# Memory-augmented recurrent transformer with an MLP on one core: TensorE's unit order and the planner's priorities are given per place in a block

## The chip, the cores and the metric

The kernel runs on one core of one Trainium2 chip. The metric is the device time of one launch in microseconds (us). All times below are us unless they are marked ns.

## What is computed

The sequence has 2048 tokens of width 512 in 64 segments of 32 tokens. Each segment is attended to together with 8 memory rows, and the attention's output in these rows is the memory of the next segment, so the segments run one after the other. Then comes an MLP with residuals.

```python
def _A_ref(x, mem0, Wq, Wk, Wv, Wo, seg_len):        # x 1x2048x512, 32 heads of 128, 8 memory rows
    mask = (idx[:, None] < M) | (idx[:, None] >= idx[None, :])
    mem = mem0
    for s in range(n_seg):                            # 64 segments of 32 tokens
        h = jnp.concatenate([mem, xs], axis=1)        # 40 rows
        q, k, v = (jnp.einsum('btd,dhe->bhte', h, W) for W in (Wq, Wk, Wv))
        scores = jnp.where(mask, jnp.einsum('bhqe,bhke->bhqk', q, k) * scale, -1e9)
        o = jnp.einsum('bhqk,bhke->bhqe', _softmax(scores), v)
        o = jnp.einsum('bhte,hed->btd', o, Wo)
        mem = o[:, :M, :].copy()                      # the next segment's memory
        outs.append(o[:, M:, :])

h = x + _A_ref(_layernorm(x), A_mem0, A_Wq, A_Wk, A_Wv, A_Wo, 32)
h2 = h + (gelu(_layernorm(_layernorm(h)) @ w1 + b1) @ w2 + b2)   # w1 512x1792, w2 1792x512
```

## The kernel before

All four attention weights stay in SBUF in bf16. A row tile of 32 rows holds a segment's first 24 tokens and the 8 memory rows (pack A, tile hT); the last 8 tokens of four segments make another tile of 32 rows (pack B, tile hB). A *block* is four segments. Pack B of a block does not depend on the memory and is projected during the block before.

TensorE (PE) works in *units*. A projection pass, for instance Q0 (the first 16 heads of Q), is four units, one for each 128 of the 512 input columns; each unit is four matmuls that run side by side in four column tiles. Where two units in a row use the same columns of the same pack, the second leaves its weight loads out (those matmuls have line 453, the others 703). The parts of a segment and their lines:

| part | what | line |
|---|---|---|
| Q0, Q1, K0, K1, V0, V1 | projections of pack A, four units each | 703 or 453 |
| SC0, SC1 | scores of the rows that need memory or last tokens (the recurrent path) | 870 |
| PV0, PV1 | their probabilities times V | 901, 905 |
| SA, PVA | scores of the first 24 tokens, and their probabilities times V one segment later | 932, 962 |
| WO | output projection, eight units; units 0 to 3 read heads of PV0, 4 to 7 of PV1 | 990 |
| F0, F1 | filler that the recurrence does not wait for: pack B of the next block (K, Q, V at block positions 0, 1, 2), at position 3 the output projection of pack B (line 1019), in the last block the first products of the MLP (line 1140) | 703, 1019, 1140 |

Around them, ScalarE (ACT) and VectorE (DVE) copy results out of PSUM (kq, VS, OT, lines 721 and 722), DVE transposes (KALL and QT, line 746), and the softmax of SC runs as reduction (nmc, L879, DVE), Exp (EC, L883, ACT), reciprocal (rsc, L886), product (PC, L889) and transpose (PTC, L890, all DVE). After WO, DVE transposes the result (TT, L1002) and adds its halves into the next segment's hT (L996). The softmax of SA has lines 942 to 951.

A planner in the kernel sets the order. Every instruction is recorded with its reads and writes and an estimated duration. PE's order is written by hand: `ORDER` is a list of (part, first unit, end unit), the same for every segment from 1 on; segment 0 has its own list `START`. For the other engines, `Sched.schedule` goes through all instructions by rank (the longest estimated path to the end) plus a number from the table `BONUS` for the kind of tile written, and gives each the earliest gap on its engine. A copy that DVE or ACT can do goes to the one that would be done first. Waits come from the dependences; each engine then runs its list in order.

```python
ORDER = (("Q0", 0, 4), ("K0", 0, 4), ("Q1", 0, 4), ("K1", 0, 2), ("SC0", 0, 99), ("K1", 2, 4), ("V0", 0, 4), ("V1", 0, 2), ("SC1", 0, 99),
         ("V1", 2, 4), ("PVA", 0, 99), ("PV0", 0, 99), ("F0", 0, 2), ("WO", 0, 4), ("PV1", 0, 99), ("F0", 2, 4), ("WO", 4, 8), ("F1", 0, 4),
         ("SA", 0, 99))
```

`START` has two fillers ("W", 7, 8) of eight 512 column matmuls each (line 672) between the WO units of segment 0. The WO weights come in eight pieces, the last of the weight loads on SP's queue (line 630).

The MLP (phase 2) goes through four blocks of 512 tokens. Its first layer starts during the last block of segments: `w1_first` computes rows of it, some of them copied raw to SBUF and put through Gelu later (`gelu_late`, line 1154). `p2_norm` (L1091, DVE) normalizes a block of h, `p2_T` transposes it by DMA, `p2_res` (L1097, POOL) adds b2 to h. The blocks' inputs are loaded back from h_mid. Nothing but the reuse of the attention's weight buffers holds the norms and b2 sums of the first two MLP blocks back.

Of the kernel before, what the change touches and what calls it, by code (L numbers as in the profile page):

```python
# [32 lines left out]
HALVES = ("kq", "KA", "QT", "ZCm", "VS", "nmc", "EC", "rsc", "PC", "PTC", "OTm", "KB", "QTB", "VSB")  # L33
BONUS = {"": 40, "EC0": -0.86, "EC1": 0.35, "KA0": -40, "KA1": 2.87, "KB0": -40, "OTB": -0.07, "OTm0": 0.99, "OTm1": -3.04, "OTx": -40, "PA": -19.24,
# [18 lines left out]
START = (("B", "V", 0, (0, 6), (1, 7)), "V", "Y", "X", ("B", "V", 1, (0, 6), (1, 7)), ("B", "K", 0, (0, 4), (1, 6)), "K0", "K1", ("B", "K", 1, (0, 4), (1, 6)),
         ("B", "Q", 0, (0, 5)), "Q0", ("B", "Q", 0, (1, 4)), "Q1", "Z", "SC0", "SC1", ("B", "Q", 1, (0, 5)), "PV0", "PV1", "SA", "WO", ("T", "WO", 0, 2),
         ("B", "Q", 1, (1, 6)), ("T", "WO", 2, 4), ("W", 7, 8), ("T", "WO", 4, 6), ("W", 7, 8), ("T", "WO", 6, 8))


class Op:
    __slots__ = ("eng", "fn", "reads", "writes", "idx", "gidx", "deps", "sig", "sigcount", "waits",
                 "tag", "pad", "held", "name", "is_dma", "dma_sem", "dur", "mode", "alone", "rank", "start", "succ", "prev", "ni", "dma_count", "alts", "kind", "occ", "kb")  # L60

    def __init__(self, eng, fn, reads, writes, name, dur, mode):
        self.eng, self.fn, self.reads, self.writes = eng, fn, reads, writes
        self.name, self.dur, self.mode = name, dur, mode
# [12 lines left out]


class Sched:
# [391 lines left out]
def build_kernel(nc, A_x, A_mem0, A_Wq, A_Wk, A_Wv, A_Wo, B_w1, B_b1, B_w2, B_b2, out):  # L471
# [3 lines left out]
    with st:  # L475
# [446 lines left out]
        def sa_mm(s, bank):  # L922
# [165 lines left out]
        def p2_norm(k):  # L1088
            for t in range(TBS):
                tb = k * TBS + t  # L1090
                S.op("dve", lambda e, tb=tb, t=t: e.tensor_scalar(xn2[:, k % 2, t, :], hx_of(k)[:, t, :], agg2[:, tb, 0:1], rst2[:, tb:tb + 1], ALU.subtract, ALU.mult),  # L1091
                     reads=[("hx", k % 2), ("ag2", tb), ("rs2", tb)], writes=[("xn4", bf_of(k), t)], after=used["WV"], dur=0.4)

        def p2_res(k):

            for t in range(TBS):
                S.op("pool", lambda e, t=t: e.tensor_tensor(hb[:, k % 2, t, :], hx_of(k)[:, t, :], b2bc[:], ALU.add), reads=[("hx", k % 2), "b2bc"],  # L1097
                     writes=[("hb", k % 2, t)], after=used["WV"] + (S.users([("rs2", NTB - 1)]) if k else []), dur=1.1)

# [35 lines left out]
        def w1_first(fc, bank, raw=False):  # L1135
# [14 lines left out]

        def gelu_late(fc):
            g, gkeys = gT0_home[fc // 2]
            g = g[:, fc % 2, :]
            S.op("act", lambda e: e.activation(g, g, ACTF.Gelu_apprx_tanh, bias=b1t[:, fc:fc + 1], scale=1.0),
                 reads=["b1t"], writes=[("gT0", fc)] + gkeys, after=exps, dur=0.66)

# [322 lines left out]
```

## Time and profile before

| | us |
|---|---|
| median of 3 runs | 842.88 |
| lowest, highest | 841.43, 843.8 |
| the profiled execution | 842.46 |
| its span, first to last instruction | 840.7 |
| PE busy, DVE busy, ACT busy, POOL busy | 800.1, 577.3, 554.3, 91.6 |

The profile is of one execution. An instruction's row gives its start (from the span's start), its duration, engine, line, operation and the tiles (written <- read), then in brackets idle time of the engine just before it and what ended it. Rows with x16 merge 16 instructions. PEld are weight loads. Ends of matmuls are modelled and overlap the next start, so the start-to-start distances tell what a unit takes. A row of a stretch (A:B) gives its length and the busy time of PE, PEld, DVE, ACT and POOL with instruction counts, then the TensorE clock granted, the busy share of the DMA engines and GB/s.

### The profile page before, as it was taken

To read this page: it belongs to the slowest core of one execution; us is meant where nothing else is said; L and a number is where in the kernel's file an instruction comes from. 1 tells how busy PE (TensorE), PEld (TensorE's weight loads), DVE (VectorE), ACT (ScalarE), POOL (GpSimd) and SP (SyncE) were. 2 spreads that over 40 slices of the span, in tenths; PEclk is the share of its full clock that TensorE was granted. 3 is DMA by queue.
4 is the path that set the end of the run, shared out by engine and by line. 5 is a ranking of instruction groups with operands and counts; after the bars stand their busy time and mean duration, and the time that the engine had idled before them with its cause. 6 is when DMAs were issued, how large, how long until landed. Compare 5 with 4: busy or idle time off the path is not lost.

```text
span 840.7 us, 46469 instructions
## 1 busy us (share of the span) xinstructions
PE 800.1 (95%) x21625; PEld 396.3 (47%) x20613; DVE 577.3 (69%) x1920; ACT 554.3 (66%) x1504; POOL 91.6 (11%) x211
## 2 busy tenths in 40 slices
PE   3788999999999999999999999999999999999998
PEld 1344544445545445445444444444545454444443
DVE  3267778878787878787878787878787877742111
ACT  2546676777677777777767777777777776672332
POOL 5012000101010101010100101000000000102500
PEclk9999999999999999999999999999999999999999
DMA  9952010101010110101010101010121130274200
GB/s 345 388 158 23 4 35 5 44 15 35 24 36 24 28 32 26 33 23 36 23 36 25 35 25 35 18 29 25 41 44 35 37 98 11 69 196 94 76 26 25
DMA packets 66946, 48.75 MB, mean 58 GB/s; under 512 B 28980, under 2 KB 63164, under 8 KB 66748
## 3 DMA queue, kind: packets, MB, share of 16 engines
q1 hardware_dynamic: 66416, 45.50, 19.0%
q8 instruction: 165, 2.70, 1.4%
q14 instruction: 33, 0.27, 0.1%
q10 hardware_dynamic: 332, 0.27, 0.1%
HBM read 31.08 MB, written 8.13 MB: 47 GB/s over the span
## 4 chain that ended last, share of the span: by engine, by line
PE 79%; DVE 11%; ACT 4%; DMA 3%; SPq 2%; issue 1%; DVEq 0%
PE ps L703 35%; PE ps L990 11%; PE ps L453 7%; PE quad L1357 6%; PE ps L1350 4%; PE quad L901 3%; PE ps L1019 3%; DMA WQ<-in_A_Wq_dram 2%; SPq L615 2%; PE quad L962 2%; PE quad L870 2%; PE ps L932 2%; DVE opT L996 2%; DVE PC L889 1%; PE ps L870 1%
## 5 line engine op out<-in xcount | busy, mean ns | idle before, releaser
L990 PE MATMUL ps<-WO,OT 128*32 128x256 bf16 x4224 | 140.3, 274 | 3.2 <-ACT OT L721 1.5
L990 PEld LDWEIGHTS ps<-WO,OT 128*32 128x32 bf16 x4224 | 103.8, 96 | 52.3 <-ACT VS L721 26.6
L721 ACT CAST OT<-quad 128x128 bf16<-128x128 f32 (+1 forms) x130 | 68.3, 526 | 87.5 <-PE quad L905 86.9
L703 PE MATMUL ps<-WQ,hT 128*32 128x512 bf16 x1796 | 121.3, 383 | 3.4 <-DVE hT L996 3.2
L721 ACT CAST kq<-ps 128x512 bf16<-128x512 f32 x162 | 94.7, 585 | 42.1 <-PE ps L703 41.4
L703 PE MATMUL ps<-WK,hT 128*32 128x512 bf16 x1544 | 117.0, 379 | 0.0
L703 PE MATMUL ps<-WV,hT 128*32 128x512 bf16 x1528 | 116.8, 380 | 0.0
L722 ACT ACTIVATE kq<-ps 128x512 bf16<-128x512 f32 x160 | 94.5, 591 | 17.7 <-PE ps L703 17.1
L721 ACT CAST VS<-ps 128x512 bf16<-128x512 f32 x127 | 74.8, 589 | 12.9 <-PE ps L703 11.0
L768 POOL COPY ZC<-QTB 128x256 bf16<-128x256 bf16 x64 | 28.3, 442 | 498.3 <-PE ps L870 360.1
L746 DVE STREAM_TRANSPOSE KALL<-kq 128x256 f32<-128x256 f32 x160 | 69.0, 438 | 14.6 <-ACT kq L721 8.2
L1002 DVE STREAM_TRANSPOSE TT<-ps 128x256 f32<-128x256 f32 x66 | 29.7, 450 | 67.8 <-PE ps L990 66.4
L703 PEld LDWEIGHTS ps<-WQ,hT 128*32 128x32 bf16 x1796 | 44.7, 97 | 50.4 <-issue 20.9
L703 PEld LDWEIGHTS ps<-WV,hT 128*32 128x32 bf16 x1528 | 36.8, 97 | 56.1 <-issue 42.7
L703 PEld LDWEIGHTS ps<-WK,hT 128*32 128x32 bf16 x1544 | 38.0, 97 | 53.2 <-issue 39.5
L1353 ACT ACTIVATE WQ<-ps,b1t 128x512 bf16<-128x512 f32 x42 | 28.9, 687 | 49.9 <-PE ps L1350 49.9
L746 DVE STREAM_TRANSPOSE QT<-kq 128x256 f32<-128x256 f32 x128 | 56.4, 440 | 4.4 <-ACT kq L722 4.3
L453 PE MATMUL ps<-WV,hT 128*32 128x512 bf16 x520 | 51.3, 382 | 0.0
L944 ACT ACTIVATE SA<-SA 128x256 f32<-128x256 f32 x64 | 26.7, 417 | 35.9 <-DVE SA L943 35.9
L453 PE MATMUL ps<-WK,hT 128*32 128x512 bf16 x504 | 49.8, 379 | 0.0
L1420 DVE TENSOR_TENSOR WV<-quad,WV 128x512 bf16<-128x512 f32 x16 | 11.1, 691 | 54.4 <-PE quad L1357 54.4
L889 DVE TENSOR_TENSOR PC<-EC,rsc 128x128 bf16<-128x128 f32 x128 | 40.1, 313 | 4.3
(156 smaller groups left out, 1377.9 us busy)
## 6 DMA issues: line engine op xcount, KB each, us to landing
WV<-in_A_Wv_dram SPq DMA_DIRECT2D x4, 1024.0 KB, 10.4
WK<-in_A_Wk_dram SPq DMA_DIRECT2D x4, 1024.0 KB, 15.8
WQ<-in_A_Wq_dram SPq DMA_DIRECT2D x4, 1024.0 KB, 22.1
WO<-in_A_Wo_dram SPq DMA_DIRECT2D x8, 512.0 KB, 9.4
v_last<-VSB SPq DMA_DIRECT2D x60, 64.0 KB, 2.5
VBD<-v_last SPq DMA_DIRECT2D x60, 64.0 KB, 3.1
h_mid<-xr SPq DMA_DIRECT2D x16, 128.0 KB, 1.7
WQ<-h_mid SPq DMA_DIRECT2D x4, 512.0 KB, 4.3
```

What stands on the lines that cost most here:

```text
L453: return e.add_instruction(mybir.InstMatmult(name="I-%d" % (4000000 + _kept[0]), engine=mybir.EngineType.PE, start_tensor_calc=start, stop ...
L703: ins = e.matmul(o, l, m, start=(k == 0), stop=(k == DC - 1), tile_position=(0, 32 * j), skip_group_check=True)
L721: return {"act": (lambda e: e.copy(out, src), t_act(n, ps_)), "dve": (lambda e: e.tensor_copy(out, src), 0.16 + 1.042e-3 * n * fast)}
L722: return {"act": (lambda e: e.mul(out, src, scale_), t_act(n, ps_)), "dve": (lambda e: e.tensor_scalar(out, src, scale_, None, ALU.mult), ...
L746: S.op("dve", lambda e: e.transpose(out, src), reads=[("kq", i)], writes=[key], dur=t_dve(256) + 0.02, after=after)
L768: S.op("pool", lambda e: e.tensor_copy(dst, src), reads=[("QTB", bk % 2, q) for q in range(2)], writes=[("ZCb", par)], dur=0.45)
L889: S.op("dve", lambda e: e.tensor_tensor(PC[:, r].rearrange("p t a -> p a t"), EC[:, r], bc, ALU.mult), reads=[("EC", r), ("rsc", r)], writ ...
L990: ins = e.matmul(ps[bank][32 * j:32 * j + 32, 0:256], lhs(slot(h)), wo_cols(h, b), start=(k == 0), stop=(k == 15), tile_position=(0, 32 * ...
L1002: S.op("dve", lambda e: e.transpose(tt.rearrange("p c q t -> p (c q t)"), ps[bank][:, 0:256]), reads=[("ps", bank)], writes=[("TT", par)], ...
L1350: ins = e.matmul(ps[bank][:, 0:SBT], W1[:, cc, fc * P:(fc + 1) * P], hnT_of(k)[:, cc, :], start=(cc == 0), stop=(cc == DC - 1))
L1353: S.op("act", lambda e: e.activation(gT[:, fc, :], ps[bank][:, 0:SBT], ACTF.Gelu_apprx_tanh, bias=b1t[:, fc:fc + 1], scale=1.0), reads=[(" ...
L1357: S.op("pe", lambda e: e.matmul(quad[:, t, :], gT_of(k, fc)[:, t * P:(t + 1) * P], W2[:, fc, :], start=(fc == 0), stop=(fc == FC - 1)), re ...
```

## The change

- `ORDERS` gives PE's unit order for each place: segments 1 to 3 (a1 to a3), the four positions in a block for all later ones (m0 to m3), and the last four segments (z60 to z63). `ORDER` remains for the order of recording and for the direction in which a pass goes through the columns. A word such as K1.0.1 is units 0 to 1 of K1.
- `BONUS` may have a key with the position in the block ("EC0@2"), which goes before the plain one.
- `START` loses its two fillers.
- `p2_norm` now waits for the last segment's second PTC, `p2_res(0)` for the last PTA.
- The first late Gelu is planned with `TABLE` = 1.28 for the load of its table, and every other Gelu of the first MLP block comes after it. The planned duration of the product into PA becomes 0.418.
- `solo` is added and used by no instruction.

```diff
+TABLE = 1.28
...
-BONUS = {"": 40, "EC0": -0.86, "EC1": 0.35, "KA0": -40, "KA1": 2.87, "KB0": -40, "OTB": -0.07, "OTm0": 0.99, "OTm1": -3.04, "OTx": -40, "PA": -19.24,
...
+BONUS = {"": 1.48, "EC0": -6.96, "EC0@0": 40, "EC0@1": -40, "EC0@2": -4.22, "EC0@3": -16.94, "EC1": -5.94, "EC1@0": 1.8, "EC1@1": 8.6,
...
+ORDERS = {"a1": "Q0.0.2 K1.0.1 Q1.0.1 K0.0.1 Q0.2.4 K0.1.4 Q1.1.4 K1.1.3 SC0.0.1 K1.3.4 V1.0.1 SC0.1.2 V0.0.1 V1.1.2 V0.1.3 SC1.0.1 V1.2.4 V0.3.4 PVA.0.2 PV0.0.1 SA.0.1 WO.0.2 PV1.0.1 WO.2.8",
...
+          "m0": "Q0.0.3 K0.0.2 Q0.3.4 K0.2.4 Q1.0.4 K1.0.1 V1.0.1 K1.1.4 V0.0.1 SC0.0.1 V0.1.2 V1.1.2 V0.2.3 F0.0.1 V0.3.4 F0.1.2 SC1.0.1 V1.2.4 PVA.0.2 PV0.0.1 F0.2.4 WO.0.2 PV1.0.1 WO.2.8 SA.0.1 F1.0.4",
+          "m1": "K0.0.1 Q0.0.2 K0.1.2 Q0.2.4 Q1.0.1 K0.2.4 Q1.1.4 K1.0.1 V1.0.1 K1.1.3 SC0.0.1 K1.3.4 V0.0.3 V1.1.2 V0.3.4 V1.2.4 SC1.0.1 PVA.0.2 F0.0.1 PV0.0.1 F0.1.4 WO.0.2 PV1.0.1 WO.2.8 F1.0.3 SA.0.1 F1.3.4",
+          "m2": "Q0.0.2 K0.0.2 Q0.2.4 Q1.0.1 K0.2.4 Q1.1.3 K1.0.1 Q1.3.4 V1.0.1 K1.1.4 SC0.0.1 V0.0.3 V1.1.4 V0.3.4 SC1.0.1 F0.0.3 PVA.0.2 PV0.0.1 F0.3.4 F1.0.1 WO.0.2 PV1.0.1 WO.2.8 F1.1.3 SA.0.1 F1.3.4",
+          "m3": "Q0.0.4 K0.0.3 Q1.0.1 K0.3.4 Q1.1.3 K1.0.1 Q1.3.4 K1.1.4 SC0.0.1 V1.0.1 V0.0.3 V1.1.2 V0.3.4 SC1.0.1 V1.2.3 PVA.0.2 V1.3.4 F1.0.1 PV0.0.1 F1.1.4 WO.0.1 PV1.0.1 WO.1.8 F1.4.5 SA.0.1 F1.5.8",
...
-         ("B", "Q", 1, (1, 6)), ("T", "WO", 2, 4), ("W", 7, 8), ("T", "WO", 4, 6), ("W", 7, 8), ("T", "WO", 6, 8))
+         ("B", "Q", 1, (1, 6)), ("T", "WO", 2, 4), ("T", "WO", 4, 6), ("T", "WO", 6, 8))
...
+        o.key = "%s@%d" % (o.kind, self.tag[0] % 4) if self.tag is not None else o.kind
...
-            heapq.heappush(heap, (-o.rank - BONUS.get(o.kind, 0.0), pos[o], o.gidx, o))
+            heapq.heappush(heap, (-o.rank - BONUS.get(o.key, BONUS.get(o.kind, 0.0)), pos[o], o.gidx, o))
...
+def place(s):
+    return "a%d" % s if s < 4 else "z%d" % s if s >= NS - 4 else "m%d" % (s % 4)
...
-                     reads=[("hx", k % 2), ("ag2", tb), ("rs2", tb)], writes=[("xn4", bf_of(k), t)], after=used["WV"], dur=0.4)
+                     reads=[("hx", k % 2), ("ag2", tb), ("rs2", tb)], writes=[("xn4", bf_of(k), t)], after=used["WV"] + ended[:1], dur=0.4)
...
-                     writes=[("hb", k % 2, t)], after=used["WV"] + (S.users([("rs2", NTB - 1)]) if k else []), dur=1.1)
+                     writes=[("hb", k % 2, t)], after=used["WV"] + (S.users([("rs2", NTB - 1)]) if k else ended[1:]), dur=1.1)
...
-                 reads=[("ps", bank), "b1t"], writes=[("gT0", fc)] + gkeys, after=exps, dur=0.69)
+                 reads=[("ps", bank), "b1t"], writes=[("gT0", fc)] + gkeys, after=exps + gelus[:1], dur=0.69)
...
-                 reads=["b1t"], writes=[("gT0", fc)] + gkeys, after=exps, dur=0.66)
+                     reads=["b1t"], writes=[("gT0", fc)] + gkeys, after=exps + gelus[:1], dur=0.66 if gelus else 0.66 + TABLE)
...
-            for n, lo, hi in ORDER:
+            for n, lo, hi in [(u, int(x), int(y)) for u, x, y in (w.split(".") for w in ORDERS.get(place(s), "").split())]:
+                S.take((s, n), lo, hi)
+            for n, lo, hi in () if place(s) in ORDERS else ORDER:
...
+        ended = [S.last_writer[("PTC", 1)], S.last_writer[("PTA", (NS - 1) % 2)]]
```

More of the change, by code (lines that the diff above doesn't have):

```diff
@@ L33 @@
 HALVES = ("kq", "KA", "QT", "ZCm", "VS", "nmc", "EC", "rsc", "PC", "PTC", "OTm", "KB", "QTB", "VSB")
-BONUS = {"": 40, "EC0": -0.86, "EC1": 0.35, "KA0": -40, "KA1": 2.87, "KB0": -40, "OTB": -0.07, "OTm0": 0.99, "OTm1": -3.04, "OTx": -40, "PA": -19.24,
[5 rows of a table removed]
-         "maskL": -25.32, "maskR": -3.79, "nma": 4.32, "nmc1": 1.11, "oBn": -40, "oN": 40, "oNr": 40, "ob": 1.25, "opA": -40, "opT0": 10.87,
-         "out": -40, "ps": -0.1, "rs": -7.71, "rs2": -9.36, "rsa": -40, "rsc0": 3.37, "sma": -40, "st": -40, "vd": 40, "xT": -1.73, "xn": -15.57,
-         "xn4": 40, "xr": 5.19}
+BONUS = {"": 1.48, "EC0": -6.96, "EC0@0": 40, "EC0@1": -40, "EC0@2": -4.22, "EC0@3": -16.94, "EC1": -5.94, "EC1@0": 1.8, "EC1@1": 8.6,
[29 rows of a table added]
 LEAN = 0.36
@@ L54 @@
          ("B", "Q", 0, (0, 5)), "Q0", ("B", "Q", 0, (1, 4)), "Q1", "Z", "SC0", "SC1", ("B", "Q", 1, (0, 5)), "PV0", "PV1", "SA", "WO", ("T", "WO", 0, 2),
-         ("B", "Q", 1, (1, 6)), ("T", "WO", 2, 4), ("W", 7, 8), ("T", "WO", 4, 6), ("W", 7, 8), ("T", "WO", 6, 8))
+         ("B", "Q", 1, (1, 6)), ("T", "WO", 2, 4), ("T", "WO", 4, 6), ("T", "WO", 6, 8))
 class Op:
     __slots__ = ("eng", "fn", "reads", "writes", "idx", "gidx", "deps", "sig", "sigcount", "waits",
-                 "tag", "pad", "held", "name", "is_dma", "dma_sem", "dur", "mode", "alone", "rank", "start", "succ", "prev", "ni", "dma_count", "alts", "kind", "occ", "kb")
+                 "tag", "pad", "held", "name", "is_dma", "dma_sem", "dur", "mode", "alone", "solo", "rank", "start", "succ", "prev", "ni", "dma_count", "alts", "kind", "key", "occ", "kb")
     def __init__(self, eng, fn, reads, writes, name, dur, mode):
@@ L66, in __init__ @@
         self.tag = self.pad = self.held = None
-        self.sig = self.is_dma = self.alone = False
+        self.sig = self.is_dma = self.alone = self.solo = False
         self.sigcount = 0
@@ L279, in finalize @@
                     cand[p.eng] = p.idx
-            if o.idx > 0 and self.streams[E][o.idx - 1].alone:
+            if o.idx > 0 and (self.streams[E][o.idx - 1].alone or o.solo):
                 cand[E] = o.idx - 1
@@ L949, in sa_mm @@
             S.op("dve", lambda e: e.tensor_tensor(PA[:].rearrange("p a t b -> p a b t"), SA[:].rearrange("p (a b) t -> p a b t", b=2), bc2, ALU.mult),
-                 ["SA", "rsa"], ["PA"], dur=0.43)
+                 ["SA", "rsa"], ["PA"], dur=0.418)
             S.op("dve", lambda e: e.transpose(PTA[:, par].rearrange("p a t b -> p (a t b)").bitcast(F32), PA[:].rearrange("p a t b -> p (a t b)").bitcast(F32)),
@@ L1148, in w1_first @@
             S.op("act", lambda e: e.activation(g, ps[bank][:, 0:SBT], ACTF.Gelu_apprx_tanh, bias=b1t[:, fc:fc + 1], scale=1.0),
-                 reads=[("ps", bank), "b1t"], writes=[("gT0", fc)] + gkeys, after=exps, dur=0.69)
+                 reads=[("ps", bank), "b1t"], writes=[("gT0", fc)] + gkeys, after=exps + gelus[:1], dur=0.69)
+        gelus = []
         def gelu_late(fc):
@@ L1153, in gelu_late @@
             g = g[:, fc % 2, :]
-            S.op("act", lambda e: e.activation(g, g, ACTF.Gelu_apprx_tanh, bias=b1t[:, fc:fc + 1], scale=1.0),
-                 reads=["b1t"], writes=[("gT0", fc)] + gkeys, after=exps, dur=0.66)
+            o = S.op("act", lambda e: e.activation(g, g, ACTF.Gelu_apprx_tanh, bias=b1t[:, fc:fc + 1], scale=1.0),
+                     reads=["b1t"], writes=[("gT0", fc)] + gkeys, after=exps + gelus[:1], dur=0.66 if gelus else 0.66 + TABLE)
+            gelus.append(o)
         def gT_of(k, fc):
```

40 rows, old and new, of tables (BONUS, ORDERS) are left out of this document.

## The prediction

> **What bounds the kernel now.** I read the page first (one core, clock at full nearly throughout), then the list of waits, then the stretch of the steady blocks, then one segment instruction by instruction on TensorE and on the two engines that feed it, and last the two ends.
>
> ```profile
> span 840.7 us, 46469 instructions
> ```
>
> ```profile
> PE ps L703 <- DVE hT L996: 3.2, 4, 1.0
> ```
>
> ```profile
> 84.95:691.58 606.63, 598.64 (x18369) 301.94 (x17507) 476.99 (x1636) 439.86 (x1246) 49.58 (x120) 1.00 0.12 31
> ```
>
> The profiled execution took 842.46 us, span 840.7 and 1.8 around it; it lies 0.4 under the median of 842.88. The stretch runs from the first Q pass of segment 4 to that of segment 60, fourteen blocks of four segments: 43.33 us a block. PE counts as busy for 598.64 of it, which leaves 8.0 of idle, but busy ends are modelled, so short waits hide in it. They show in the distance from one start to the next. Segment 409.74 to 420.36 on PE, with ellipses, and of two other segments the second score product (L870 into ps) and the second PV (the later L901):
>
> ```profile
> 403.94 0.31 PE L870 MATMUL ps<-KALL,ZC 128*32 128x64 bf16 x16
> ...
> 406.95 0.27 PE L901 MATMUL quad<-PTC,VS 32*128 32x16 bf16 x16 [0.20 <-DVE PTC L890]
> ...
> 409.74 1.05 PE L703 MATMUL ps<-WQ,hT 128*32 128x512 bf16 x16
> ...
> 412.88 0.30 PE L870 MATMUL quad<-KALL,ZC 128*32 128x64 bf16 x16
> ...
> 414.78 0.30 PE L870 MATMUL ps<-KALL,ZC 128*32 128x64 bf16 x16
> 414.91 0.60 PE L703 MATMUL ps<-WV,hT 128*32 128x512 bf16 x8
> 415.45 0.37 PE L962 MATMUL quad<-PTA,VS 32*128 32x32 bf16 x32
> ...
> 415.97 0.62 PE L703 MATMUL ps<-WV,hB 128*32 128x512 bf16 x8
> 416.54 1.06 PE L990 MATMUL ps<-WO,OT 128*32 128x256 bf16 x32
> 417.64 0.26 PE L901 MATMUL quad<-PTC,VS 32*128 32x16 bf16 x16
> ...
> 417.88 0.61 PE L703 MATMUL ps<-WV,hB 128*32 128x512 bf16 x8
> 418.33 1.06 PE L990 MATMUL ps<-WO,OT 128*32 128x256 bf16 x32
> 419.21 1.04 PE L703 MATMUL ps<-WV,hB 128*32 128x512 bf16 x16
> 420.07 0.42 PE L932 MATMUL ps<-KALL,QT 128*32 128x32 bf16 x32
> 420.36 1.05 PE L703 MATMUL ps<-WQ,hT 128*32 128x512 bf16 x16
> ...
> 436.45 0.30 PE L870 MATMUL ps<-KALL,ZC 128*32 128x64 bf16 x16
> ...
> 439.56 0.27 PE L901 MATMUL quad<-PTC,VS 32*128 32x16 bf16 x16 [0.20 <-DVE PTC L890]
> ```
>
> Prices from it. A pass of four units (419.21 to 420.07) is 0.86, so 0.2155 a unit. A score product is 0.13 (414.78 to 414.91). Half of WO (four units, 418.33 to 419.21) is 0.88. SA is 0.29. Going from column tiles to row tiles costs 0.11: two V units need 0.43 and took 0.54 (414.91 to 415.45). PVA, PV0 and the way back to column tiles are 0.52 (415.45 to 415.97). F0 before WO took 0.57 for two units: 0.14 of wait for OT. WO before PV1 took 1.10 for 0.88: 0.11 for the tiles, 0.11 of wait for PTC.
>
> PV1 is where the segment is decided. It came 2.86 after its score product in this segment, 3.01 in the one before and 3.11 in the one at block position 0. Why so long, on DVE and ACT:
>
> ```profile
> 413.24 0.29 DVE L879 TENSOR_REDUCE nmc<-quad 128x2 f32<-128x128 f32 x1
> ...
> 415.42 0.25 DVE L890 STREAM_TRANSPOSE PTC<-PC 128x64 f32<-128x64 f32 x1
> ...
> 415.57 0.58 ACT L721 CAST VS<-ps 128x512 bf16<-128x512 f32 x1 [0.24 <-PE ps L703]
> 415.59 0.25 DVE L879 TENSOR_REDUCE nmc<-ps 128x2 f32<-128x128 f32 x1
> ...
> 416.05 0.32 ACT L883 ACTIVATE EC<-ps,nmc 128x64 f32<-128x64 f32 x1
> ...
> 419.92 0.39 DVE L996 TENSOR_TENSOR hT<-TT 64x32 bf16<-64x32 f32 x2
> ```
>
> The reduction of score 0 began 0.36 after its product (412.88, 413.24); that of score 1 began 0.81 after, right behind the last instruction of softmax 0 (415.42): 0.45 of queue on DVE. Its Exp began 0.21 after the reduction's end, while ACT copied VS: 0.21 of queue on ACT. Without both the latency would be 2.20. And after WO, TT and hT take DVE to 420.31, 0.05 before the next Q0: WO's end to Q0 is 1.15 (419.21 to 420.36), and no filler on PE shorter than that helps.
>
> **The change part by part: the steady blocks.** From PV1 to the next Q0 stand PV1 0.24 (417.64 to 417.88), the WO units left, and 1.15. Before: two F units, 0.45, and half of WO, 0.88: 2.72. New: positions 0, 1 and 2 keep six WO units of 0.22 behind PV1, 0.24 + 1.32 + 1.15 = 2.71; position 3 keeps seven and a whole F pass, 0.24 + 1.54 + 0.86 + 0.29 = 2.93. Nothing gained there. Position 2 has moved one F unit ahead of PV1, and its filler of 0.94 falls short of the 1.15, which is in the 2.71.
>
> Before PV1 things move. Score 1 stood behind 22 projection units; in positions 0, 1 and 2 it stands behind 24 units and score 0, 24 x 0.2155 + 0.13 = 5.30 after Q0 (before 5.04 at 414.78, 0.17 of it wait); in position 3 behind 22, 4.87. Score 0 moves from 14 units to 18, 16, 17 and 16. In exchange the K1 copies have six to eight units and score 0 for cover before score 1 where they had six units, so score 1 does not wait; and K1 and Q1 are transposed before or just after score 0, no longer between it and its softmax. So a segment is, with L from score 1 to PV1:
> - positions 0, 1, 2: 5.30 + L + 2.71 = 8.01 + L each
> - position 3: 4.87 + L + 2.93 = 7.80 + L, and 0.10 for TensorE's slow stretch at WOB, which I leave where it is
> - block: 31.93 + 4 L. The present 43.33 corresponds to L = 2.85.
>
> L is not to be read before the change; the ends are 2.20 (no queue) and 3.11 (position 0 now). I take 2.70: 2.20, plus 0.21 because V copies still end around score 1, plus 0.29, one instruction of softmax 0 of the size of its reduction in front where there were several. It is nearest to the 2.86 row, whose DVE queue it shortens and whose ACT queue it keeps. Block: 42.73, 0.60 less, times 14: 8.4 us. PE itself permits this: in position 0, 28 projection units 6.03, two WO units 0.44, two products 0.26, PVA and PV0 0.52, two tile changes 0.22 and the OT wait 0.14 put PV1 at 7.61 after Q0 at the earliest, where L = 2.70 puts it at 8.00. Positions 1 and 3 now have PVA, PV0 and PV1 apart, two more tile changes each, 0.21, but three units before WO and so no OT wait; that lies in this slack.
>
> The last block (segments 60 to 62) has the same shapes: 0.15 a segment, 0.4. Segments 1 to 3 have no F; three of the four waits for hT (3.2 us) are theirs, and the new orders put six to eight WO units behind PV1. I take nothing, with 1.5 either way. The longer table of priorities, keyed by place, adds no instruction: it decides the DVE and ACT order, which is L. TABLE and 0.418 are numbers of the planner alone.
>
> **The end of the recurrence** (norms and b2 sums held back):
>
> ```profile
> 731.88 1.38 DVE L1091 TENSOR_SCALAR WV<-WQ,agg,rst 128x512 bf16<-128x512 bf16 x4 [0.63 <-DMA WQ<-h_mid]
> ...
> 733.18 4.55 POOL L1097 TENSOR_TENSOR WV<-WQ,b2bc 128x512 f32<-128x512 bf16 x4 [20.33 <-DMA WQ<-h_mid]
> ...
> 733.37 1.11 DVE L889 TENSOR_TENSOR PC<-EC,rsc 128x128 bf16<-128x128 f32 x1
> ...
> 734.82 0.27 PE L901 MATMUL quad<-PTC,VS 32*128 32x16 bf16 x16 [1.38 <-DVE PTC L890]
> ...
> 739.48 1.28 ACT L1154 ACT_TABLE_LOAD   x1
> ...
> 742.12 1.20 ACT L721 CAST VSB<-ps 128x512 bf16<-128x512 f32 x2
> ...
> 742.76 1.90 PE L1140 MATMUL ps<-hnT,VBD 128*128 128x512 bf16 x8 [1.11 <-ACT VSB L721]
> ```
>
> Four norms of the MLP (1.38) sat on DVE ahead of the last softmax, and its product then took 1.11 while POOL ran the b2 sums; so much of the wait of 1.38 hangs on them that I book all of it. The norms go behind PTC, and with them their four transposing DMAs on SP's queue and the weight pieces after those; the sums go behind PTA, with them the next load of h_mid. Cover: the MLP of block 1, for which both are made, starts over 20 us later. If SP's queue stood, the weights of W2 would be late, and they have some 10 us. Then 1.11 of wait for two copies that queue behind the table load and two Gelus: with the load counted the planner can put the copies first. I take 0.6 of 1.11 (ends 0 and 1.11). Together 2.0, ends 1.0 and 2.5.
>
> **The start** (two fillers of eight matmuls dropped):
>
> ```profile
> L630 SPq DMA_DIRECT2D WO<-in_A_Wo_dram x8: 1415/1924/4758, 21.1 to 40.3; - x8
> DMA to landing us min/median/max: 9.0/9.4/13.2
> ```
>
> ```profile
> L672 PE MATMUL ps<-WV,ident x16: 378/379/390, 47.4 to 51.3; 128*128 128x512 bf16 x16
> ```
>
> ```profile
> 51.58 0.62 PE L990 MATMUL ps<-WO,OT 128*32 128x256 bf16 x16
> 53.19 1.05 PE L703 MATMUL ps<-WQ,hT 128*32 128x512 bf16 x16 [0.98 <-DVE hT L996]
> ```
>
> ```profile
> 40.09:43.51 3.42, 1.54 (x58) 0.65 (x52) 2.25 (x10) 3.04 (x14) 0.40 (x1) 1.00 1.10 349
> 43.51:46.92 3.41, 3.25 (x89) 2.22 (x93) 2.22 (x7) 1.21 (x4) 0.00 (x0) 0.50 1.12 351
> ```
>
> The last piece of WO lands at 40.3 + 9.0 = 49.3; the last two WO units ran at 51.58, behind the second filler. Without fillers they can run at 49.35, 2.23 sooner, and Q0 1.61 later, at 50.96. But a stretch of 3.41 with PE busy for 1.54 was followed by one at clock 0.50. Without fillers 46.92 to 50.33 would hold some 1.5 of work as well (three pairs of WO units), so half clock until 53.74, and the 2.8 us of passes in it cost 1.4. Net 0.8; ends 2.2 gained and 0.5 lost. [...]
>
> Sum: 842.46 - 8.4 - 0.4 - 2.0 - 0.8 = 830.9; outside the steady blocks it is 3.2.
>
> **Rivals.**
> - *The two softmaxes collide* (slower). Score 0 stood 1.90 before score 1 (412.88, 414.78); now 1.42 in positions 0 and 3, 1.85 in 1 and 1.64 in 2. If softmax 0 keeps its pace, the reduction of score 1 queues as long as now, while score 1 itself comes 0.26 later. With L at the mean of the three rows, 2.99, a block is 43.89, 7.8 us more in all: 847. It decides from L = 2.91, where the 3.2 are used up. For: DVE 79% and ACT 73% busy in the stretch. Against: the transposes of Q1 and K1 that lengthened softmax 0 go out of its way.
> - *No queue left.* Then PE's own order bounds: PV1 at 7.61, 7.68, 7.83 (29 units) and 7.46 (one WO unit), segments 10.32, 10.39, 10.54 and 10.49, a block 41.74, 22.3 us less: 817. For: PE alone is at its price nearly everywhere. Against: each copy on ACT is 0.58 and some will stand in the way.
> - *The order on PE doesn't matter.* DVE, not PE's order, sets when softmax 1 ends; L grows by what score 1 saves. The blocks stay at 43.33, only the ends gain: 839.3.
>
> **How the numbers follow.** Forecast 0.50 at 831, own range 824 to 837 (0.1 of L is 5.6 us); collision 0.15 at 847; no queue 0.17 at 817; no matter 0.18 at 839. The range 816 to 847 leaves out about half of the two outer cases. A measurement of this kernel can tell 0.3%, 2.5 us, from no change: under 840.4 is faster, over 845.4 slower. Faster: the forecast, the case without queue, and half of no matter, 0.76; same 0.11; slower 0.13.
>
> **What would show it.** The stretch from segment 4 to 60 near 598 us; no wait at score 0 or 1; the distance from score 1 to PV1 near 2.7 (above 2.9 the prediction is wrong, and DVE rows between score 1 and its reduction would show why); in the last segment PC at about 0.3 and no wait before PV1; WO's last units near 49.4 and a stretch of half clock after 50.3; the copies before 742 ahead of the table load.

## The result, and the profile after

The changed kernel takes 823.04 us (median of four runs, 820.84 to 823.9); the kernel before, run beside it, 843.34 (841.43 to 844.15). The ratio is 0.9758, with a 95% interval of 0.9733 to 0.9784. The forecast was 831 with 816 to 847. The profiled execution took 823.39.

The page of the kernel after, first line, then its stretches: segments 1 to 3, the fourteen steady blocks, segments 60 to 62, and from segment 63 to the second group of products with W2, the one that reads hT (called W2 below).

```profile
span 821.7 us, 46520 instructions
```

```profile
51.67:90.73 39.06, 32.55 (x893) 17.17 (x901) 26.00 (x81) 21.97 (x68) 8.56 (x22) 0.85 0.13 28
90.73:672.18 581.45, 580.12 (x18368) 314.87 (x17445) 488.09 (x1551) 450.56 (x1328) 47.08 (x119) 1.00 0.13 32
672.18:705.72 33.54, 31.08 (x911) 16.82 (x877) 26.02 (x83) 25.90 (x74) 1.60 (x4) 1.00 0.11 29
705.72:734.95 29.23, 26.44 (x557) 14.29 (x561) 17.05 (x44) 19.68 (x40) 4.97 (x4) 0.94 0.48 141
```

The same stretches of the kernel before, beside the steady one that the prediction shows:

```profile
53.19:84.95 31.76, 26.75 (x892) 14.06 (x841) 24.95 (x84) 21.09 (x62) 8.47 (x22) 1.00 0.25 30
691.57:725.04 33.47, 32.79 (x919) 15.83 (x864) 25.16 (x87) 23.42 (x66) 1.70 (x4) 1.00 0.09 24
725.04:754.00 28.96, 25.88 (x588) 13.19 (x551) 17.10 (x49) 21.29 (x44) 4.55 (x4) 1.00 0.60 164
```

| stretch | before | after | difference | forecast |
|---|---|---|---|---|
| up to Q0 of segment 1 | 53.19 | 51.67 | -1.5 | -2.2, then +1.4 for half clock |
| segments 1 to 3 | 31.76 | 39.06 | +7.3 | 0 |
| fourteen steady blocks | 606.62 | 581.45 | -25.2 | -8.4 |
| segments 60 to 62 | 33.47 | 33.54 | +0.1 | -0.4 |
| segment 63 to W2 | 28.96 | 29.23 | +0.3 | -2.0 |

A block fell from 43.33 to 41.53 us, three times the gain forecast; in the steady stretch PE is busy for 580.12 of 581.45. All four other lines of the table gained less than forecast or lost, by 9.4 in sum.

TensorE of the kernel after, a segment at block position 2 (second and third row, L908: scores 0 and 1; fourth, L939: PV1), and before it Q0, score 1 and PV1 of one at position 0:

```profile
381.45 0.83 PE L741 MATMUL ps<-WQ,hT 128*32 128x512 bf16 x12
...
386.76 0.29 PE L908 MATMUL ps<-KALL,ZC 128*32 128x64 bf16 x16
...
389.10 0.26 PE L939 MATMUL quad<-PTC,VS 32*128 32x16 bf16 x16
...
402.17 0.61 PE L741 MATMUL ps<-WQ,hT 128*32 128x512 bf16 x8
...
405.85 0.29 PE L908 MATMUL quad<-KALL,ZC 128*32 128x64 bf16 x16
...
407.48 0.29 PE L908 MATMUL ps<-KALL,ZC 128*32 128x64 bf16 x16
...
409.87 0.26 PE L939 MATMUL quad<-PTC,VS 32*128 32x16 bf16 x16
...
412.60 1.05 PE L741 MATMUL ps<-WQ,hT 128*32 128x512 bf16 x16
```

Score 1 comes 5.31 after Q0, PV1 2.34 (position 0) and 2.39 (position 2) after score 1, and the next Q0 2.73 after PV1. The softmaxes of the segment at position 2, on DVE and ACT:

```profile
407.87 0.29 DVE L917 TENSOR_REDUCE nmc<-ps 128x2 f32<-128x128 f32 x1
408.08 0.23 DVE L928 STREAM_TRANSPOSE PTC<-PC 128x64 f32<-128x64 f32 x1
408.20 0.32 ACT L921 ACTIVATE EC<-ps,nmc 128x64 f32<-128x64 f32 x1
408.24 0.65 DVE L759 CAST VS<-ps 128x512 bf16<-128x512 f32 x1
...
409.47 0.24 DVE L928 STREAM_TRANSPOSE PTC<-PC 128x64 f32<-128x64 f32 x1
...
412.16 0.39 DVE L1034 TENSOR_TENSOR hT<-TT 64x32 bf16<-64x32 f32 x2
```

The reduction of score 1 starts 0.39 after its product (before 0.81): it now goes ahead of the last transpose of softmax 0, and the Exp starts 0.04 after it (before 0.21), because the second V copy went to DVE, behind the transpose. 0.42 and 0.17 are the two queues, and they make 0.59 of the 0.66 that the prediction had as the most that could go.

The start of the kernel after: the last WO units, Q0 of segment 1, and four stretches of 3.41 or 3.42 (the clock is the figure after POOL's):

```profile
49.64 1.05 PE L1028 MATMUL ps<-WO,OT 128*32 128x256 bf16 x16 [1.99 <-DMA WO<-in_A_Wo_dram]
51.67 1.04 PE L741 MATMUL ps<-WQ,hT 128*32 128x512 bf16 x8 [0.98 <-DVE hT L1034]
```

```profile
46.22:49.63 3.41, 1.30 (x36) 0.72 (x29) 1.14 (x3) 0.60 (x1) 0.00 (x0) 1.00 0.87 280
49.63:53.04 3.41, 2.42 (x32) 1.09 (x36) 2.19 (x6) 0.00 (x0) 0.31 (x2) 0.50 0.51 141
59.87:63.28 3.41, 2.35 (x140) 1.73 (x136) 2.41 (x9) 1.65 (x8) 0.89 (x4) 1.00 0.21 43
63.28:66.70 3.42, 2.45 (x48) 1.42 (x44) 2.22 (x7) 1.36 (x3) 0.50 (x2) 0.50 0.02 5
```

Half clock lasted from 49.63 to 56.46 and again from 63.28 to 70.11, four stretches of 3.41 or 3.42 instead of the one forecast.

The tail of the kernel after: TensorE in segment 63, SP's two loads of h_mid, then the DMA queues between 704.40 and 712.96 with the page's line of queue q8:

```profile
715.42 0.33 PE L970 MATMUL ps<-KALL,QT 128*32 128x32 bf16 x19 [2.31 <-issue]
...
708.75 0.83 SPq L1123 DMA_DIRECT2D WQ<-h_mid  x2
```

```profile
q1 hardware_dynamic: 242, 0.93, 33.4%
```

```profile
q8 instruction: 165, 2.70, 1.3%
```

The wait of 1.38 before PV1 is gone, and PE stands 2.31 in the middle of SA instead, between two of its 32 matmuls, with nothing awaited ("issue"). Queue q8 carried 165 packets, 2.70 MB, 16 KB each; PE and PEld ran 42,226 instructions in all, 256 for each packet, so I read q8 as TensorE's program. The traces bear this out. In all runs together PE stops 24 times for over 0.3 with "issue" as what ended it. Counted over all rows of PE and PEld, each of these stops comes 186 to 195 rows past a multiple of 256 (the traces miss some records: for the same products PE has 21,609 rows before, without the 16 of the fillers, and 21,593 after), and PE goes on 2.2 to 2.9 after a packet of q8 has started. So I read these stops as PE waiting for its next 256 instructions. Here the packet started 8.56 after the one before (704.40 and 712.96), and the two loads of 512 KB were issued at 708.75, about half way.

### The profile page after: what moved, and what is told of

Its sections match the earlier page's. It is cut to its first block, busy times and chain, and to the rows that moved or that the text cites. A ratio compares the mean times of both kernels' runs of the same rounds, so it can differ in the third digit from the quotient of the medians.

```text
span 821.7 us, 46520 instructions
## 1 busy us (share of the span) xinstructions
PE 781.2 (95%) x21593; PEld 412.7 (50%) x20633; DVE 590.6 (72%) x1826; ACT 566.9 (69%) x1598; POOL 88.0 (11%) x211
## 4 chain that ended last, share of the span: by engine, by line
PE 88%; SPq 5%; DVE 3%; ACT 2%; issue 1%; DMA 1%; DVEq 0%
PE ps L741 42%; PE ps L1028 15%; PE ps L491 7%; PE quad L1400 6%; PE ps L1393 4%; PE ps L1057 3%; PE quad L939 3%; SPq L653 2%; SPq L668 2%; PE quad L1000 2%; PE ps L1178 1%; PE ps L970 1%; DVE TT L1040 1%; DMA WO<-in_A_Wo_dram 1%; DVE hT L1034 1%
## 5 line engine op out<-in xcount | busy, mean ns | idle before, releaser
L741 PE MATMUL ps<-WK,hT 128*32 128x512 bf16 x1812 | 141.6, 385 | 1.4 <-DVE hT L1034 1.3
L741 PE MATMUL ps<-WQ,hT 128*32 128x512 bf16 x1760 | 131.3, 385 | 5.2 <-DVE hT L1034 3.9
L1028 PEld LDWEIGHTS ps<-WO,OT 128*32 128x32 bf16 x4224 | 101.3, 97 | 30.7 <-DVE rsc L924 8.8
L741 PE MATMUL ps<-WV,hT 128*32 128x512 bf16 x1512 | 112.8, 380 | 0.0
L759 ACT CAST OT<-quad 128x128 bf16<-128x128 f32 (+1 forms) x190 | 84.4, 444 | 29.8 <-PE quad L943 24.7
L741 PEld LDWEIGHTS ps<-WK,hT 128*32 128x32 bf16 x1812 | 49.2, 98 | 78.6 <-issue 35.9
L806 POOL COPY ZC<-QTB 128x256 bf16<-128x256 bf16 x64 | 25.6, 401 | 498.5 <-PE ps L908 473.2
L759 ACT CAST VS<-ps 128x512 bf16<-128x512 f32 x82 | 47.9, 587 | 9.2 <-PE ps L741 6.7
L491 PE MATMUL ps<-WV,hT 128*32 128x512 bf16 x536 | 52.5, 380 | 0.0
L921 ACT ACTIVATE EC<-ps,nmc 128x64 f32<-128x64 f32 x130 | 39.8, 311 | 7.2 <-DVE nmc L917 5.3
L741 PE MATMUL ps<-WQ,hB 128*32 128x512 bf16 x512 | 40.1, 389 | 3.8 <-DMA WQ<-in_A_Wq_dram 3.8
```

Of the source, the lines that this page charges most:

```text
L491: return e.add_instruction(mybir.InstMatmult(name="I-%d" % (4000000 + _kept[0]), engine=mybir.EngineType.PE, start_tensor_calc=start, stop ...
L741: ins = e.matmul(o, l, m, start=(k == 0), stop=(k == DC - 1), tile_position=(0, 32 * j), skip_group_check=True)
L759: return {"act": (lambda e: e.copy(out, src), t_act(n, ps_)), "dve": (lambda e: e.tensor_copy(out, src), 0.16 + 1.042e-3 * n * fast)}
L921: ins = e.activation(EC[:, r, sl, :], o[:, 64 * sl:64 * sl + 64], ACTF.Exp, bias=nmc[:, r, sl:sl + 1], accum_out=smc[:, r, sl:sl + 1])
L1028: ins = e.matmul(ps[bank][32 * j:32 * j + 32, 0:256], lhs(slot(h)), wo_cols(h, b), start=(k == 0), stop=(k == 15), tile_position=(0, 32 * ...
```

## The experiments

The theory after the result: the table of priorities took the queue out of softmax 1 because it was made for these unit orders, so order and table are one unit; PE's own order bounds the blocks now; the start and segments 1 to 3 lose to their orders and to half clock; the tail loses to late instruction packets. The rivals: the order alone, or the table alone, gives the gain; PE without fillers is the whole loss of the start; the holds (norms, sums) are what matters in the tail. Ratios are against the kernel before, whose median was about 843 in all comparisons.

### The orders with the old table

```diff
-BONUS = {"": 1.48, "EC0": -6.96, "EC0@0": 40, ...
+BONUS = {"": 40, "EC0": -0.86, "EC1": 0.35, ...
```

> The changed kernel with the new unit orders but the old table of priorities. Steady block (segments 4 to 60, divided by 14): 43.33 us before, 41.5 after. Theory 'place': what shortens L (from the second score product to PV1) is where the score products stand on TensorE, which takes the transposes of Q1 and K1 out of the way of softmax 0; then L stays near 2.4 to 2.5 and the block near 41.6 to 42. Theory 'queue': it is the priorities that put the second reduction ahead of softmax 0's last transpose and the Exp ahead of the V copies; then L stays near 2.85 to 3.0, the block near 43.3 to 43.9, and all of the gain is gone.

922.36 us, 1.0937 (1.0907 to 1.0966). A block takes 48.08, longer than either theory had it. The two largest of TensorE's waits in the steady blocks (waited for, us in total, times, longest), and a second score product:

```profile
PE ps L720 <- DVE hT L1013: 47.9, 49, 1.3
PE ps L887 <- ACT ZC L777: 35.0, 33, 1.7
```

```profile
458.25 0.40 DVE L763 STREAM_TRANSPOSE QT<-kq 128x256 f32<-128x256 f32 x1
459.06 0.30 PE L887 MATMUL ps<-KALL,ZC 128*32 128x64 bf16 x16 [1.16 <-ACT ZC L777]
```

The distance from score 1 to PV1 is short here too (2.40 to 2.74), but the transpose of Q1 comes only behind softmax 0, so score 1 itself is late, and hT queues on DVE behind SA's softmax, so Q0 is late. The order shifts the queue, it does not empty it.

### The table with the old order

```diff
-ORDERS = {"a1": "Q0.0.2 K1.0.1 Q1.0.1 K0.0.1 ...", ...
+ORDERS = {}          # so every segment from 1 on takes ORDER
```

> The changed kernel with the old unit order everywhere and the new table of priorities. Theory 'place': L stays near 2.85 and the block near 43.3. Theory 'queue': L goes to 2.4 to 2.5; as the second score product stands earlier in the old order, PE's own order then bounds, with PV1 at 7.6 after Q0 and a block near 41.6. Whatever the blocks do, segments 1 to 3 have their old order, and should take near 10.6 each at full clock.

892.42 us, 1.0582 (1.0546 to 1.0618); a block 46.55, again longer than either theory had it. Segments 1 to 3 took 36.38 with their old order, at half clock up to 56.7, and not the 31.8 expected. Three of TensorE's largest waits:

```profile
PE ps L898 <- DVE PTC L918: 18.9, 31, 0.8
PE quad L898 <- DVE KALL L774: 9.7, 30, 0.5
PE ps L1018 <- ACT OT L749: 9.3, 33, 0.8
```

The products of score 0 and 1 (L898) now wait for DVE, and WO (L1018) for OT. Neither half, put beside the old other half, gives any of the gain; each then costs 50 to 80 us.

### No priorities at all

```diff
-BONUS = {"": 1.48, ...
+BONUS = {}
```

> The changed kernel with an empty table of priorities: the planner goes by its estimated paths alone. With the old table the new orders gave a block of 48.1 us (12.44, 11.70, 11.02, 12.93 for positions 3, 0, 1, 2 as the segments come), because hT stood on DVE behind the reductions of SA and the transpose of Q1 behind softmax 0. Theory 'any order needs its own table': without one the block is about as long as with the wrong one or a little better, 43 to 48. Rival 'the old table did harm, the new one little good': the block is near 41.5 to 42 without any.

842.39 us, 0.9986 (0.9967 to 1.0005). With the new orders and the bare ranks a block takes 43.07, and score 1 to PV1 takes 2.65, 2.72, 2.66 and 2.79 at the four positions: the 2.70 of the forecast. The block is 0.34 longer than the 42.73 forecast with it; nearly all of that is score 1 at position 1, 5.60 after Q0 where 5.30 was forecast. The PV products (L910 here) wait again, as before the change:

```profile
PE quad L910 <- DVE PTC L899: 8.9, 29, 0.8
```

The table, given the orders, is worth the difference to the kernel after, 1.54 a block or 21.6 us over fourteen.

### The table without its place keys

```diff
-BONUS = {"": 1.48, "EC0": -6.96, "EC0@0": 40, "EC0@1": -40, ...
+BONUS = {"": 1.48, "EC0": -6.96, ...          # keys with "@" taken out; also the loads of h_mid in pieces, as below
```

> The changed kernel with split h_mid loads and with the new table less its keys for a position in the block: every kind of tile has one number again. With the whole table L was 2.30 to 2.53 and the block 41.5, with none 2.65 to 2.79 and 43.06. Theory 'the place keys carry it': L goes to 2.6 or more and the block to 43 or more. Rival 'one number per kind is enough': the block stays within 41.5 to 42.2.

952.77 us, 1.1307 (1.128 to 1.1333); a block 50.19.

```profile
PE ps L879 <- ACT ZC L769: 59.2, 46, 1.7
PE ps L712 <- DVE hT L1005: 40.0, 18, 2.9
```

The plain entries alone are far worse than none, so they do not stand by themselves. That they were made only beside the place keys is my reading; no run shows how the table was made.

### The fillers of the start put back

```diff
-         ... ("T", "WO", 2, 4), ("T", "WO", 4, 6), ("T", "WO", 6, 8))
+         ... ("T", "WO", 2, 4), ("W", 7, 8), ("T", "WO", 4, 6), ("W", 7, 8), ("T", "WO", 6, 8))
```

> The changed kernel with the two fillers in segment 0 put back. After the change segments 1 to 3 took 14.6, 13.2 and 11.3 us (before 10.6 each), with half clock from 49.6 to 56.5 and from 63.3 to 70.1. Theory 'fillers': they kept the clock up; then Q0 of segment 1 comes 1.5 later (near 53.2) but no half clock follows 47, segments 1 to 3 take near 11 each, and the whole gains 4 to 5 us. Theory 'orders of segments 1 to 3': these orders leave PE idle often enough to lower the clock again whatever came before; then a stretch of half clock remains after 60 and the gain is under 2 us.

823.05 us, 0.9751 (0.9725 to 0.9778): no difference to the kernel after (0.9758). Its segments 1 to 3:

```profile
52.78:86.77 33.99, 27.45 (x892) 15.74 (x901) 26.10 (x81) 21.84 (x68) 8.54 (x22) 1.00 0.16 31
```

At full clock throughout they take 33.99, against 31.76 before the change: 2.2 is lost to the orders of segments 1 to 3 with this table. The other 5.1 of the kernel after's 7.3 came with half clock, and differ between executions: the same start and orders without fillers took 34.2 to 37.2 in other kernels below. So the 5.1 saved here are one execution against another. Three other stretches took 4.2 of them back: Q0 came 1.1 later, the fourteen blocks took 1.7 longer (583.15, with one stop of 1.28 for an instruction packet), and the tail 1.4 (30.63).

### The loads of h_mid in pieces

```diff
-            S.dma(lambda e: e.dma_start(hx_of(k), hd[:, k * TBS:(k + 1) * TBS, :]), 512, ...
+            for t in range(TBS):
+                S.dma(lambda e, t=t: e.dma_start(hx_of(k)[:, t, :], hd[:, k * TBS + t, :]), 128, ...
```

> The changed kernel with each load of a block of h_mid (512 KB) as four loads of 128 KB, one after the other. After the change PE stood for 2.31 us inside SA of the last segment, with no wait on another engine, while the 16 KB packets of PE's own instructions came 8.6 us apart (704.4, 713.0) instead of some 4, and two 512 KB loads of h_mid were issued at 708.75. Theory 'fetch': the instruction packet stood behind these loads; with small loads the packet comes in time, the 2.31 and the half clock behind it (715.2 to 718.6) go, and the whole gains 2.3 to 3.5 us. Rival: the stall is PE's own (a block of instructions that begins inside SA); then it stays and nothing is gained.

818.36 us, 0.9717 (0.9681 to 0.9754). This interval meets that of the kernel after, so the stage has to tell. TensorE in segment 63, SP's eight loads of h_mid, and the stretch to W2:

```profile
710.83 0.30 PE L970 MATMUL ps<-KALL,QT 128*32 128x32 bf16 x19 [0.67 <-issue]
...
705.80 9.28 SPq L1124 DMA_DIRECT2D WQ<-h_mid  x8
```

```profile
702.77:729.50 26.73, 25.86 (x560) 13.82 (x561) 18.78 (x44) 19.67 (x40) 4.66 (x4) 1.00 0.51 150
```

The packet now starts 7.04 after the one before it. The stop at the same matmul falls from 2.31 to 0.67, the half clock behind it (0.94 in the kernel after's stretch) goes, and the stretch takes 26.73 instead of 29.23; against the 28.96 of the kernel before that is the 2.0 forecast for the tail, and 0.2 more.

Of the kernels with whole loads, five stop for 1.3 to 2.5 in the last segment, and the old order with the new table for 0.62 and 0.35; those with pieces stop for 0.67 or less. That the loads delay the packet is shown by the edit (7.04 from one packet to the next, where the kernel after has 8.56). But the pieces also go out one behind the other, eight over 9.28 where the two whole loads went out in 0.83, so it is open whether their size or their spacing helps, and on which resource loads and packets meet.

Loads of h_mid are not the only cause: in the steady blocks PE stopped once for 1.29 here, and once for 1.28 with the fillers put back, both times for a packet that started 5.6 to 5.8 after the one before, with only smaller transfers under way (four of 64 KB, issued 3.7 and 3.8 before the packet). What delayed these two is not shown. The stretch to W2 is what the edit gives; two other stretches of this execution differ from the kernel after without any edit to them: segments 1 to 3 took 34.21 at full clock in this execution, and the blocks 2.2 longer.

### The holds taken out

```diff
-    after=used["WV"] + ended[:1], dur=0.4)
+    after=used["WV"], dur=0.4)
...
-    ... if k else ended[1:]), dur=1.1)
+    ... if k else []), dur=1.1)
```

With the loads in pieces:

> The changed kernel with split h_mid loads, the norms of the MLP and the b2 sums no longer held back. From Q of segment 63 to the end of its PV1 the recurrence has the norms (1.4) and slower products next to POOL's sums in its way again. Theory of the prediction: PV1 waits about 1.4 longer, the whole is 1.4 to 2 us slower than with the holds. Rival: with loads that come one by one the norms cannot start before PTC anyway, and nothing changes (under 0.5).

819.95 us, 0.9738 (0.9694 to 0.9782), against 0.9717 with the holds; from segment 63 to W2 both take 26.73. The norms start at 720.79, long after the last PTC at 711.76, without any hold: with this table and the loads in pieces they are out of the way by themselves, and the holds then do nothing that shows. Which of the two does it is not separated.

### The tail of the change alone, on the kernel before

```diff
+TABLE = 1.28
...        # the holds, the order of the Gelus and TABLE, as in the change; nothing else of it
```

> The kernel before with the three edits at the end alone: norms and b2 sums held back, the late Gelus ordered, the table load planned. The prediction's step gives 2.0 us less (ends 1.0 and 2.5), with no wait for PTC before PV1 of segment 63. Rival 'the fetch takes its place': the instruction packet of PE stood behind the h_mid loads before the change too (724.07 and 732.55 were 8.5 apart), so PE waits there about as long without the norms, inside a unit and for no engine, and the whole changes by less than 0.7.

841.65 us, 0.9985 (0.9975 to 0.9994): 1.35 gained of the 2.0, by the interval 0.5 to 2.1. Segment 63 to W2 went from 28.96 to 27.66. PV1 of the last segment:

```profile
734.56 0.19 PE L902 MATMUL quad<-PTC,VS 32*128 32x16 bf16 x5 [1.33 <-issue]
```

PTC is there, and PV1 stops all the same, after 11 of its 16 matmuls, for 1.33: here too no instruction packet came for 7.85 us (724.34 to 732.19). The copies now run ahead of the table load (740.73 and 743.06), and the wait of 1.11 for them is gone, so the second half of the tail step held and gave more than the 0.6 taken. The first half gave next to nothing, and the trace before shows why. There the packet started at 732.55; with the 2.37 that passed here from the packet's start to PV1 going on, its instructions are there at about 734.9 (my estimate), and PTC came at 734.76. By this estimate the wait for PTC lay over a wait for instructions that was there without it.

### Score 1 two units later

```diff
-  "m0": "... F0.1.2 SC1.0.1 V1.2.4 PVA.0.2 ..."
+  "m0": "... F0.1.2 V1.2.4 SC1.0.1 PVA.0.2 ..."
```

Loads in pieces, position 0 alone:

> The changed kernel with split h_mid loads; at block position 0 alone the second score product stands behind the last two V units in place of ahead of them (5.74 after Q0, not 5.31). It measures the floor of L, which was 2.33 at this position with PV1 at 7.64 and TensorE never waiting for PTC. Theory 'floor 2.2 as in the prediction': PV1 comes at 7.9 to 8.1, the segment takes 10.65 to 10.85 (10.39 before this edit), the other three positions stay. Rival 'TensorE's own order is the bound and L has room': PV1 stays at 7.64, L 1.9, and the segment at 10.4.

823.40 us, 0.9761 (0.9732 to 0.979). Scores and PV1 at position 0:

```profile
385.83 0.30 PE L908 MATMUL ps<-KALL,ZC 128*32 128x64 bf16 x16
...
388.11 0.26 PE L939 MATMUL quad<-PTC,VS 32*128 32x16 bf16 x16
```

Score 1 moved back by 0.43, PV1 by 0.38, and the segment grew from 10.40 to 10.77. Against the 818.36 of the loads in pieces alone the kernel is 5.0 slower, and 14 times 0.37 is 5.2. From score 1 to PV1 it is 2.28 with two units fewer between them; so the softmax cannot be much quicker, and in the kernel after PE's work up to PV1 (7.64) and the softmax (5.31 + 2.28 = 7.59) end within 0.05 of each other.

### The positions' orders in all segments, and the start

```diff
-  "a1": "Q0.0.2 K1.0.1 ...", "a2": ..., "a3": ..., "z60": ..., "z61": ..., "z62": ..., "z63": ...
+  # a1 to a3 = m1 to m3 (a1 with both units of SC0 at one place), z60 to z63 = m0 to m3; loads of h_mid in pieces
```

> The changed kernel with split h_mid loads, and with the four orders of the positions also in segments 1 to 3 and 60 to 63 in place of their own. At full clock the own orders gave 11.66, 11.27, 11.28 for segments 1 to 3 (old order: 10.6 each) and 11.0, 10.96, 11.78 for 60 to 62 (old: 11.3, 11.2, 10.9). Theory 'all of WO behind PV1 costs': orders a2 and a3 put all eight WO units behind PV1; with two in front segments 1 to 3 take 10.4 to 10.7, 2 to 3 us less in all, and 60 to 62 about 10.5, 2 to 3 us less. Rival 'the table was made for those orders': the priorities do not fit, segments 1 to 3 take 11.5 or more and nothing or a loss comes of it.

812.29 us, 0.9635 (0.9608 to 0.9662), 10.8 less than the kernel after, and 6.1 less than with the loads in pieces alone (818.36). The four stretches (segments 1 to 3, blocks, 60 to 62, 63 to W2):

```profile
51.25:82.43 31.18, 26.64 (x892) 15.20 (x847) 24.65 (x79) 21.29 (x67) 8.15 (x22) 1.00 0.22 37
82.43:663.78 581.35, 580.02 (x18368) 316.43 (x17498) 488.89 (x1553) 450.19 (x1329) 48.24 (x120) 1.00 0.14 32
663.78:696.70 32.92, 32.54 (x917) 15.99 (x857) 25.23 (x81) 25.28 (x72) 1.59 (x4) 1.00 0.13 32
696.70:722.72 26.02, 25.49 (x561) 13.64 (x545) 18.29 (x43) 19.70 (x43) 4.65 (x4) 1.00 0.53 156
```

Segments 1 to 3 take 31.18 without any filler in the start, and the clock stays full in them. Segments 60 to 62 gained 0.6 against the kernel after, where 2 to 3 were expected. Two more runs on this basis:

> The changed kernel with split h_mid loads and the positions' orders also in segments 1 to 3 and 61 to 63 (60 keeps its own, which took 10.8 where position 0 took 11.3). The version with position 0 there ran in 812.3; by that difference 811.8, so no difference that these runs can tell.

> The same with the two fillers of segment 0 put back. Theory of the prediction: dropping them moves Q0 of segment 1 forward by 1.6 and costs 0.8 of it by half clock, so with them 0.8 slower on the mean. Rival 'they only cost': with the positions' orders in segments 1 to 3 PE is busy enough to keep its clock, and with the fillers it is 1.1 to 2.2 slower. Rival 'they pay': 1 us or more faster with them.

With its own order back at segment 60: 812.58 us, 0.9648 (0.9622 to 0.9675), the same. With the fillers besides: 815.25, 0.9674 (0.9658 to 0.9689). Q0 of segment 1 comes at 54.40 instead of 51.48, and segments 1 to 3 take as long either way (31.07 and 31.16), so the 2.9 is paid and nothing comes back; the intervals overlap, the stage times are of one execution each.

## Why the prediction was right, and where it was not

- **Form of the segment: right.** Score 1 was put 5.30 after Q0 (4.87 at position 3); measured 5.31 and 4.88 over twelve blocks. From PV1 to Q0 2.71 and 2.93 were forecast; measured 2.73 to 2.75, and 2.94. The first is the price of the 24 units and score 0, so score 1 waits for nothing there, as forecast.
- **L, score 1 to PV1: the term that was mis-sized.** 2.70 was taken; measured 2.33, 2.30, 2.39 and 2.53. The step that failed is "0.21 because V copies still end around score 1, plus 0.29, one instruction of softmax 0": both queues went, the one because a V copy went to DVE behind the reduction, the other because the reduction goes ahead of softmax 0's transpose. The prediction called the table "the DVE and ACT order, which is L" and then left 0.50 of the 0.66 of queue in place. With no table L is 2.65 to 2.79, so 2.70 was the price of the orders with untuned priorities.
- **The rival without queue came true in the blocks.** It had PV1 at 7.61, 7.68, 7.83 and 7.46 and a block of 41.74; measured 7.64, 7.61, 7.71, 7.41 and 41.53. The rest of that rival, 817, took the ends as forecast, and these failed. The collision (L of 2.91 or more) fell at every position. "The order on PE doesn't matter" is close to what the orders gave without priorities (a block of 43.07), not to what the change gave.
- **Segments 1 to 3: wrong by 7.3.** "I take nothing" was too little: 2.2 are the orders a1 to a3 with this table, 5.1 half clock in the profiled execution, and with the positions' orders the same segments take 31.18.
- **The start: wrong in how often the clock fell.** WO's last units ran at 49.64 (forecast 49.35), Q0 at 51.67 (50.96). One stretch of 3.41 at half clock was counted; four came, two from 49.63 and two from 63.28. The second pair followed a stretch in which PE, between the PV products and WO of segment 1, was busy for 2.35 of 3.41; that the first pair caused it is not shown.
- **The tail: right on what goes, wrong on what is late next.** The norms and sums left the path, PC took 0.30, the copies no longer hold PE. One sign did not come: the table load (720.92) is still ahead of the copies (723.01), whose wait went all the same. The step that failed is "so much of the wait of 1.38 hangs on them that I book all of it", and with it the cover, which named the MLP and W2's weights and not TensorE's own program: PE stood there until an instruction packet had come, whether norms were in the way or not (1.33 on the kernel before, 2.31 after the change). So the -2.0 became +0.3; with the loads in pieces it is -2.2.

So 831 against 823 is two errors that partly cancel: the forecast gave the blocks 16.8 too little gain and the rest 9.4 too much. That the total lies well inside 816 to 847 is luck to that extent; it is just outside the 824 to 837 that the forecast gave itself, between it and the rival without queue.

## What to carry to other kernels

A hand-written unit order and a table of priorities are one object: either half of this one, beside the old other half, costs 6 to 9%, the orders with no table gain nothing that shows in the whole, and a table cut to its plain keys is worse than none, so price them together and take PE's own work as a likely bound when order and table fit each other. When a wait before PE is removed, look for what PE meets next, its instruction packets behind large loads included, and spread such loads out (PE stood 2.31 here with two loads of 512 KB, 0.67 with eight of 128 KB). A filler that is to keep the clock up costs its own time (Q0 of segment 1 came 1.1 and 2.9 later with it); here it brought nothing that could be measured in the whole, and better orders in the segments after it took 31.2 for them without one, against 34.0 at full clock with the change's own.

## What the runs showed of the hardware

- Queue q8 moved 165 packets of 16 KB while PE and PEld ran 42,226 instructions, 256 for each packet, and I read them as TensorE's program. In all runs together PE stood 24 times for over 0.3 with nothing awaited, each time 186 to 195 rows past a multiple of 256, and went on 2.2 to 2.9 after a packet's start. In the last segment of the kernel after, with two loads of 512 KB issued within 0.83, the packets came 8.56 apart and PE stood 2.31 with nothing awaited. Four loads of 128 KB in place of each, spread over 9.28, left 7.04 and 0.67.
- The clock fell here after a stretch without a gap over 1.06, and stayed full after one with less work. In the stretch 59.87 to 63.28 PE was busy for 2.35 of 3.41, which leaves no gap over 1.06, and two of 3.42 and 3.41 at clock 0.50 followed. Of the times at half clock in the traces before and after, two lasted 3.41 (43.51 to 46.92 before, 715.23 to 718.64 after) and two twice that, 6.83 (49.63 to 56.46 and 63.28 to 70.11 after). But the busy time of the stretch ahead does not settle whether the clock falls. A later stretch of the same length in the same execution held less work, and the clock stayed full after it:

```profile
87.17:90.58 3.41, 2.17 (x84) 1.84 (x84) 1.30 (x5) 2.06 (x6) 0.30 (x1) 1.00 0.21 43
```

What decides besides is not shown, so no threshold of busy time can be given.
